# ScalarE instead of SP issues the store of a block's decoded weight words, behind its own cast of them

## The chip, the cores and the metric

The kernel runs on one core of one Trainium2 chip. The metric is device time of one launch in microseconds (us), the median of several runs. One more execution was taken by the hardware profiler; its rows are what this document reads.

## The reference

Attention over blocks, a gated causal convolution, a Fourier mix and a two-layer network, one after the other, for 8 batches of 576 positions and 512 channels:

```python
attn = softmax(scale * q @ k.T, block-causal mask of 64) @ v
x    = concat_heads(attn)                                   # (8, 576, 512)
x    = (sigmoid(causal_conv(x, conv_w)) * (x @ w_val)) @ w_out
mixed = real(fft(fft(x, axis=1), axis=2))
u  = x + mixed
un = (u - mean(u)) / sqrt(var(u) + 1e-6)
out = u + relu(un @ w_ch1) @ w_ch2                          # 512 -> 2048 -> 512
```

The weights come in as 64-bit floats. The kernel gets their 32-bit halves, and builds 32-bit floats from them on the chip.

## The kernel before

**Two phases.** `phase1` does attention, convolution and the Fourier mix, and writes u to DRAM (`u_d`). `phase2` does the normalization and the two-layer network. The first 1024 tokens (two groups g of 512) go through the network directly: for each of 16 blocks f of 128 hidden units, TensorE makes `psh` (12 matmuls of 512 columns, L1516 to L1518: three products of high and low parts for four slices of 128), ScalarE and VectorE turn it into `HL` (L1520 is the high part with the relu, L1521 the low part), and the 12 matmuls `o` (L1537 to L1539) add block f-1 to the output. The remaining tokens go through a scheme with fewer products, whose weight sums are built meanwhile by `combine` from the decoded blocks in DRAM.

**A block's weights.** Blocks 0 and 1 are decoded in phase 1. Blocks 2 to 15 are decoded by `load_w` while group 0 runs, with `load_raw` and `keep_base` around it:

- L1189: two loads of 512 KB bring the block's raw words (`rw`).
- L71: ScalarE makes the size of each word (`st`, 128x1024). `st` is one of three buffers.
- L75, L76, L80, L82: VectorE finishes `st`, in place.
- L1213: SP issues the store of `st` to DRAM (`w_d`, 512 KB). A buffer of `st` is free for L71 of the third block behind it when this store has landed and the block's L1216 is done.
- L1215: ScalarE casts `st` to the high parts, the first half of the block's weight tile `W`.
- L1216: VectorE makes the low parts, the other half of `W`.
- L1201: SP stores three of the four high and low pieces (`base_d`, 768 KB).

In `psh` of a block the first and second matmul of each slice need the high parts, the third (L1518) the low ones.

**What sets the order.** A scheduler decides, when the program is built, the order in which each engine's instructions stand, from its own estimate of times; every engine then works through its list in that order. SP's list holds nearly all DMAs. [...]

Of the kernel before, what the change touches and what calls it, by code (L numbers as in the profile page):

```python
# [17 lines left out]
def kernel(  # L18
# [13 lines left out]
    nc = tc.nc  # L32
# [32 lines left out]
    def decode(raw, dst, fine=False):  # L65

        lo, hi = raw[:, 0::2], raw[:, 1::2]
        d = dst.bitcast(I32)

        def size():  # L70
            nc.scalar.activation(out=dst, in_=hi.bitcast(F32), func=AF.Abs)  # L71

        def bits():

            nc.vector.tensor_scalar_max(out=dst, in0=dst, scalar1=2.0 ** -15)  # L75
            nc.vector.tensor_scalar(out=d, in0=d, scalar1=3, scalar2=0x3FFFFFFF,  # L76
                                    op0=ALU.logical_shift_left, op1=ALU.bitwise_and)

        def rest():
            nc.vector.scalar_tensor_tensor(out=d, in0=lo, scalar=29, in1=d,  # L80
                                           op0=ALU.logical_shift_right, op1=ALU.bitwise_or)
            nc.vector.scalar_tensor_tensor(out=d, in0=hi, scalar=-0x40000000, in1=d,  # L82
                                           op0=ALU.bitwise_and, op1=ALU.bitwise_or)

        def whole():
            bits()
            rest()
        return [size, bits, rest] if fine else [size, whole]
# [8 lines left out]
    w_d = [dram.tile([P, 2 * D], F32, name=f"w_d{f}") for f in range(NF)]  # L97
# [16 lines left out]
    def w_places(f, t):  # L114
        WQ[f] = [x[:, 0:D] for x in t]
# [934 lines left out]
    def phase2():  # L1050
        with ExitStack() as c2:
# [31 lines left out]
            def at(n, shape, dt, name):  # L1083
                return place[n].tile(shape, dt, tag="w", name=name)
# [120 lines left out]
            def load_w(f):  # L1205
                W = at(f, [P, 4 * D], F32R, f"W{f}")
                WW[f] = W
                w_places(f, [W[:, D * z:D * z + D] for z in range(4)])
                h, l = (W.rearrange("p (q y c) -> p q y c", y=2, c=256)[:, :, y] for y in range(2))
                st = s3.tile([P, 2 * D], F32, tag="st", name="st")  # L1210
                for stage in decode(RAW[f], st):
                    stage()
                nc.sync.dma_start(out=w_d[f], in_=st)  # L1213
                x = st.rearrange("p (q c) -> p q c", c=256)
                nc.scalar.copy(out=h, in_=x)  # L1215
                nc.vector.tensor_tensor(out=l, in0=x, in1=h.bitcast(F32), op=ALU.subtract)  # L1216

            pin = [False]
# [269 lines left out]
            for g in range(NG):  # L1488
# [4 lines left out]
                for f in range(NF + 1):  # L1493
# [3 lines left out]
                    if g == 0 and f + 2 < NF:  # L1497
                        load_raw(f + 5)
                        load_w(f + 2)
                        if f + 2 < NH:  # L1500
                            keep_base(f + 2)
# [177 lines left out]
```

## Time and profile before

| | |
|---|---|
| median of 3 runs | 1404.49 us (1403.73 to 1406.47) |
| profiled execution | 1408.24 us, its span 1406.2 us |
| TensorE (PE) busy | 1352.7 us, 96% of the span |
| VectorE (DVE) busy | 1087.7 us, 77% |
| ScalarE (ACT) busy | 821.8 us, 58% |
| store of decoded words (L1213) | 14 issues, 512 KB each, 655.4 to 757.9 us of the span |

The profiled execution is 3.75 us above the median of the runs. PE is TensorE's matmuls, PEld its weight loads, DVE VectorE, ACT ScalarE, POOL GpSimd, SP the engine that only issues. A name with q at its end (SPq) is an engine's queue of instructions that count as no busy time, such as DMA issues. "idle before" is the time that an engine stood still ahead of an instruction, with what ended it. In a list of order, a tile name ends in a number that tells one buffer's use from the next.

### The profile page before, as it was taken

The page shows a single profiled execution, that of the slowest core. Times are in us where ns is not written, and L with a number is a line of the kernel's source. Part 1 is how long each engine was busy: PE and PEld are TensorE (multiplying, and loading weights), DVE is VectorE, ACT ScalarE, POOL GpSimd, SP SyncE. Part 2 cuts the span into 40 slices and gives each one's busy share as a digit, 9 for nine tenths or more (in the row PEclk, how much of TensorE's full clock was granted, in tenths as well). Part 3 has the DMA queues.
Part 4 walks back from the last instruction along what each step waited for, and adds up shares of the span by engine and source line. Part 5 has one row for each costly group of instructions (what it writes and reads, how often), then busy time and mean ns, then how long its engine had stood idle before and what let it go on. Part 6 is the DMA issues. An engine that isn't in the chain of part 4 may idle for free.

```text
span 1406.2 us, 24032 instructions
## 1 busy us (share of the span) xinstructions
PE 1352.7 (96%) x8547; PEld 1188.0 (84%) x8547; DVE 1087.7 (77%) x1965; ACT 821.8 (58%) x1792; POOL 211.0 (15%) x186
## 2 busy tenths in 40 slices
PE   5798999999999999999999999999999999999998
PEld 3576789898999988888778788888888889999998
DVE  5867788787879797989889798599746983796374
ACT  5677867777777777774444344574356534744451
POOL 2423232323223232322200000000000000000000
PEclk9799999999999999999999999999999999999999
DMA  7566665656656566646698987985875579779875
GB/s 211 137 167 187 160 185 153 173 149 165 160 154 159 155 171 157 178 150 215 217 359 291 340 320 246 318 275 190 289 261 200 179 243 334 251 252 320 272 253 185
DMA packets 177043, 308.78 MB, mean 220 GB/s; under 512 B 28430, under 2 KB 107036, under 8 KB 169756
## 3 DMA queue, kind: packets, MB, share of 16 engines
q1 hardware_dynamic: 176096, 306.57, 69.1%
q8 instruction: 68, 1.11, 0.3%
q0 software_dynamic: 288, 0.53, 0.2%
q14 instruction: 51, 0.42, 0.1%
q10 hardware_dynamic: 540, 0.14, 0.1%
HBM read 204.27 MB, written 56.77 MB: 186 GB/s over the span
## 4 chain that ended last, share of the span: by engine, by line
PE 68%; DVE 14%; DMA 6%; ACT 4%; issue 3%; POOL 3%; SPq 1%; DVEq 0%; ACTq 0%; POOLq 0%
PE banks L1437 12%; PE banks L1438 12%; PE banks L1439 12%; PE av L616 4%; PE pt L588 4%; DVE gate L643 2%; PE sc L428 2%; POOL XA L849 2%; PE sc L429 2%; DVE mx L460 1%; PE psx L192 1%; PE psx L194 1%; PE psx L193 1%; DMA rw<-in_w_ch 1%; ACT PB L474 1%
## 5 line engine op out<-in xcount | busy, mean ns | idle before, releaser
L1437 PE MATMUL banks<-o,chunk 128*128 128x512 f32 (+1 forms) x896 | 324.2, 362 | 1.1 <-ACT h L1445 1.1
L1438 PE MATMUL banks<-o,chunk 128*128 128x512 f32 (+1 forms) x896 | 324.0, 362 | 0.0
L1439 PE MATMUL banks<-o,chunk 128*128 128x512 f32 (+1 forms) x896 | 324.0, 362 | 0.0
L474 ACT ACTIVATE PB<-sc,mx 128x128 f32<-128x128 f32 (+4 forms) x320 | 166.8, 526 | 49.6 <-DVE mx L460 27.7
L1437 PEld LDWEIGHTS banks<-o,chunk 128*128 128x128 f32 x896 | 168.2, 188 | 19.3 <-ACT h L1445 2.0
L1438 PEld LDWEIGHTS banks<-o,chunk 128*128 128x128 f32 x896 | 168.2, 188 | 17.4
L1439 PEld LDWEIGHTS banks<-o,chunk 128*128 128x128 f32 x896 | 168.2, 188 | 17.5
L1397 ACT CAST o<-h 128x1024 fp32r<-128x1024 f32 (+1 forms) x112 | 105.4, 945 | 106.9 <-PE banks L1439 86.5
L588 PE MATMUL pt<-ident,PB 128*128 128x128 f32 x800 | 142.9, 285 | 15.4 <-ACT PTb L594 8.2
L1398 DVE TENSOR_TENSOR o<-h,o 128x1024 fp32r<-128x1024 f32 (+1 forms) x112 | 119.8, 1084 | 23.6 <-ACT o L1397 23.2
L588 PEld LDWEIGHTS pt<-ident,PB 128*128 128x128 f32 x800 | 101.7, 145 | 32.5 <-ACT PTb L594 14.7
L643 DVE SCALAR_TENSOR_TENSOR gate<-XF,cw,gate 128x575 f32<-128x575 f32 (+3 forms) x128 | 122.7, 958 | 4.3 <-ACT gate L63 3.6
L460 DVE TENSOR_REDUCE mx<-sc 128x1 f32<-128x384 f32 (+2 forms) x192 | 104.3, 560 | 4.4 <-PE sc L194 2.7
L428 PE MATMUL sc<-K,QQ 128*128 128x256 f32 (+2 forms) x256 | 88.3, 355 | 14.4 <-DMA QQ<-QHL 13.5
L594 ACT COPY PTb<-pt 128x512 f32<-128x512 f32 (+1 forms) x160 | 86.7, 545 | 18.9 <-PE pt L588 18.2
L1445 ACT COPY h<-banks 128x1024 f32<-128x1024 f32 (+1 forms) x64 | 58.1, 907 | 56.9 <-PE banks L1439 56.9
L192 PE MATMUL psx<-GH,we_h 128*128 128x290 f32 x256 | 83.6, 326 | 2.5 <-ACT GH L57 1.5
L192 PE MATMUL psv<-XH,wv_h 128*128 128x288 f32 x256 | 83.8, 328 | 0.4 <-ACT PB L474 0.4
L639 POOL TENSOR_TENSOR XL<-XF,XH 128x576 fp32r<-128x576 f32 x32 | 45.9, 1434 | 251.1 <-ACT XH L57 250.9
L429 PE MATMUL sc<-KL,QQ 128*128 128x256 f32 (+2 forms) x256 | 83.3, 336 | 0.0
L193 PE MATMUL psx<-GL,we_h 128*128 128x290 f32 x256 | 76.1, 297 | 0.5 <-DVE GL L704 0.5
L193 PE MATMUL psv<-XL,wv_h 128*128 128x288 f32 x256 | 76.3, 298 | 0.0
(272 smaller groups left out, 3152.5 us busy)
## 6 DMA issues: line engine op xcount, KB each, us to landing
chunk<-comb_d SPq DMA_DIRECT2D x64, 512.0 KB, 5.8
chunk<-comb_d SPq DMA_DIRECT2D x32, 1024.0 KB, 4.8
chunk<-base_d SPq DMA_DIRECT2D x48, 512.0 KB, 5.9
chunk<-base_d SPq DMA_DIRECT2D x24, 1024.0 KB, 6.8
K<-KP SPq DMA_DIRECT2D x128, 144.0 KB, 2.5
QQ<-QHL SPq DMA_DIRECT2D x128, 128.0 KB, 2.4
rw<-in_w_ch SPq DMA_DIRECT2D x28, 512.0 KB, 8.2
comb_d<-packed SPq DMA_DIRECT2D x12, 1024.0 KB, 5.1
```

The source lines that it names most:

```text
L192: nc.tensor.matmul(ps, lh, rh, start=first, stop=False)
L193: nc.tensor.matmul(ps, lh, rl, start=False, stop=False)
L428: nc.tensor.matmul(t[:, o:o + w], q[:, 0, m], KK[p][h][:, 0:w], start=True, stop=False)
L429: nc.tensor.matmul(t[:, o:o + w], q[:, 1, m], KL[p][:, 0:w], start=False, stop=True)
L460: nc.vector.reduce_max(out=mx[:, j:j + 1], in_=t, axis=AX.X, negate=one)
L474: nc.scalar.activation(out=PB[i][:, k0:k0 + w], in_=t, func=AF.Exp, bias=nm, accum_out=su[:, at + j:at + j + 1])
L588: nc.tensor.transpose(ps[:, j, :], PB[i][:, (j0 + j) * P:(j0 + j + 1) * P], ident)
L643: nc.vector.scalar_tensor_tensor(out=gate[c][:, s:S], in0=XF[:, 0:S - s], scalar=cw[:, c, 4 - s:5 - s], in1=gate[c][:, s:S], op0=ALU.mult, ...
L1398: nc.vector.tensor_tensor(out=o[:, 1], in0=x, in1=o[:, 0].bitcast(F32), op=ALU.subtract)
L1437: nc.tensor.matmul(to, wh, o[:, 0, x], start=first, stop=False, skip_group_check=not begin)
L1438: nc.tensor.matmul(to, wh, o[:, 1, x], start=False, stop=False, skip_group_check=not begin)
L1439: nc.tensor.matmul(to, wl, o[:, 0, x], start=False, stop=last, skip_group_check=not begin)
```

## The change

The store moves from SP's list to ScalarE's, and in the program's text from ahead of the cast to behind it.

```diff
                 st = s3.tile([P, 2 * D], F32, tag="st", name="st")
                 for stage in decode(RAW[f], st):
                     stage()
-                nc.sync.dma_start(out=w_d[f], in_=st)
                 x = st.rearrange("p (q c) -> p q c", c=256)
                 nc.scalar.copy(out=h, in_=x)
+                nc.scalar.dma_start(out=w_d[f], in_=st)
                 nc.vector.tensor_tensor(out=l, in0=x, in1=h.bitcast(F32), op=ALU.subtract)
```

A line is taken out above the cast, so the cast is L1214 in the changed kernel and the store L1215. The scheduler orders all engines anew; outside this stage little moves.

First SP's list, at the raw words of blocks 10 to 14 of group 0. `w_d7` to `w_d10` are the stores of blocks 7 to 10, `rw_9629` is block 11's raw words, `rw_9669` block 12's, `rw_9709` block 13's, `rw_9749` block 14's. Before:

```order
L1213 DMA w_d7_78<-st_9592 128x1024
L1201 DMA base_d01_88<-W7_9591 128x3x512
L1189 DMA rw_9629<-in_w_ch1 128x4x256
L1189 DMA rw_9629<-in_w_ch2 128x1024
L1213 DMA w_d8_79<-st_9633 128x1024
L1189 DMA rw_9669<-in_w_ch1 128x4x256
L1189 DMA rw_9669<-in_w_ch2 128x1024
L1213 DMA w_d9_80<-st_9673 128x1024
L1189 DMA rw_9709<-in_w_ch1 128x4x256
L1189 DMA rw_9709<-in_w_ch2 128x1024
L1213 DMA w_d10_81<-st_9713 128x1024
```

And in the changed kernel:

```order
L1201 DMA base_d01_88<-W7_9591 128x3x512
L1189 DMA rw_9629<-in_w_ch1 128x4x256
L1189 DMA rw_9629<-in_w_ch2 128x1024
L1189 DMA rw_9669<-in_w_ch1 128x4x256
L1189 DMA rw_9669<-in_w_ch2 128x1024
L1189 DMA rw_9709<-in_w_ch1 128x4x256
L1189 DMA rw_9709<-in_w_ch2 128x1024
L1189 DMA rw_9749<-in_w_ch1 128x4x256
L1189 DMA rw_9749<-in_w_ch2 128x1024
```

The loads stand in the same order; the stores between them, each of which waited for VectorE, are gone.

Then ScalarE's list, at the casts of blocks 8 to 11. `st_9713` is block 10 in decoding, `st_9753` block 11, `st_9796` block 12; `psh_9682`, `psh_9722` and `psh_9765` are the first-layer sums of blocks 7, 8 and 9. Before:

```order
L1215 CAST W8_9632<-st_9633 128x4x256
L1520 ACTIVATE HL_9331<-psh_9682 128x512
L1215 CAST W9_9672<-st_9673 128x4x256
L71 ACTIVATE st_9713<-rw_9588 128x1024
L1520 ACTIVATE HL_9331<-psh_9722 128x512
L1215 CAST W10_9712<-st_9713 128x4x256
L1520 ACTIVATE HL_9331<-psh_9765 128x512
L71 ACTIVATE st_9753<-rw_9629 128x1024
L71 ACTIVATE st_9796<-rw_9669 128x1024
L1215 CAST W11_9752<-st_9753 128x4x256
```

And in the changed kernel:

```order
L1214 CAST W8_9632<-st_9633 128x4x256
L1215 DMA w_d8_79<-st_9633 128x1024
L71 ACTIVATE st_9713<-rw_9588 128x1024
L1520 ACTIVATE HL_9331<-psh_9682 128x512
L1214 CAST W9_9672<-st_9673 128x4x256
L1215 DMA w_d9_80<-st_9673 128x1024
L71 ACTIVATE st_9753<-rw_9629 128x1024
L1520 ACTIVATE HL_9331<-psh_9722 128x512
L71 ACTIVATE st_9796<-rw_9669 128x1024
L1214 CAST W10_9712<-st_9713 128x4x256
L1215 DMA w_d10_81<-st_9713 128x1024
L1520 ACTIVATE HL_9331<-psh_9765 128x512
```

Beside the stores, L71 of blocks 10, 11 and 12 has moved up: block 10's now stands ahead of the relu of block 7's sums, and block 12's ahead of the cast of block 10.

Last VectorE's list at the same place. Before:

```order
L82 SCALAR_TENSOR_TENSOR st_9713<-rw_9588,st_9713 128x1024
L1216 TENSOR_TENSOR W10_9712<-st_9713,W10_9712 128x4x256
L1521 SCALAR_TENSOR_TENSOR HL_9331<-psh_9765,HL_9331 128x512
L75 TENSOR_SCALAR st_9753<-st_9753 128x1024
L76 TENSOR_SCALAR st_9753<-st_9753 128x1024
L80 SCALAR_TENSOR_TENSOR st_9753<-rw_9629,st_9753 128x1024
L82 SCALAR_TENSOR_TENSOR st_9753<-rw_9629,st_9753 128x1024
```

And in the changed kernel:

```order
L82 SCALAR_TENSOR_TENSOR st_9713<-rw_9588,st_9713 128x1024
L1521 SCALAR_TENSOR_TENSOR HL_9331<-psh_9722,HL_9331 128x512
L75 TENSOR_SCALAR st_9753<-st_9753 128x1024
L75 TENSOR_SCALAR st_9796<-st_9796 128x1024
L1216 TENSOR_TENSOR W10_9712<-st_9713,W10_9712 128x4x256
L76 TENSOR_SCALAR st_9753<-st_9753 128x1024
L76 TENSOR_SCALAR st_9796<-st_9796 128x1024
L80 SCALAR_TENSOR_TENSOR st_9753<-rw_9629,st_9753 128x1024
L1521 SCALAR_TENSOR_TENSOR HL_9331<-psh_9765,HL_9331 128x512
L82 SCALAR_TENSOR_TENSOR st_9753<-rw_9629,st_9753 128x1024
```

The first step of blocks 11 and 12 now stands ahead of the low parts of block 10.

## Rows read from the trace of the kernel before

**Rows 1.** The profile page: the span, and the engines' busy time.

```profile
span 1406.2 us, 24032 instructions
PE 1352.7 (96%) x8547; PEld 1188.0 (84%) x8547; DVE 1087.7 (77%) x1965; ACT 821.8 (58%) x1792; POOL 211.0 (15%) x186
```

**Rows 2.** Busy time by stage: PE, PEld, DVE, ACT, POOL, clock, DMA share, GB/s.

```profile
690.00:742.00 52.00, 51.06 (x220) 40.54 (x219) 44.89 (x52) 22.93 (x26) 1.10 (x2) 1.00 1.03 354
742.00:766.00 24.00, 24.00 (x107) 19.32 (x106) 23.25 (x32) 11.47 (x17) 0.00 (x0) 1.00 0.80 275
766.00:800.00 34.00, 34.00 (x150) 27.87 (x150) 25.88 (x49) 11.00 (x16) 1.61 (x3) 1.00 0.94 325
880.00:1406.00 526.00, 521.38 (x2618) 471.46 (x2616) 368.18 (x441) 253.85 (x307) 0.00 (x0) 1.00 0.75 255
```

**Rows 3.** Timeline of PE, 660 to 810 us: the instructions with idle time ahead.

```profile
667.09 0.73 PE L1516 MATMUL psh<-UTH,K 128*128 128x512 f32 x2 [0.42 <-ACT UTH L1135]
668.24 0.50 PE L1517 MATMUL psh<-UTL,K 128*128 128x512 f32 x1 [0.41 <-DVE UTL L1136]
681.99 0.73 PE L1539 MATMUL o<-HL,KP 128*128 128x512 f32 x2 [0.56 <-DVE HL L1521]
...
729.08 0.50 PE L1518 MATMUL psh<-UTH,W 128*128 128x512 f32 x1 [0.52 <-DVE W L1216]
...
734.61 0.50 PE L1516 MATMUL psh<-UTH,W 128*128 128x512 f32 x1 [0.21 <-ACT W L1215]
735.99 0.50 PE L1518 MATMUL psh<-UTH,W 128*128 128x512 f32 x1 [0.17 <-DVE W L1216]
...
802.33 0.49 PE L1114 MATMUL pm<-ah,ones 128*128 128x512 f32 x1 [1.12 <-ACT ah L1111]
```

**Rows 4.** Waits of ACT and of SP's queue, 690 to 770 us: total, times, longest.

```profile
ACT st L71 <- DMA w_d<-st: 4.7, 3, 2.3
...
SPq L1213 <- DVE st L82: 28.0, 7, 5.8
```

**Rows 5.** The decoded words' tile w_d: issue ns min/median/max, and landing times.

```profile
L1213 SPq DMA_DIRECT2D w_d<-st x14: 319/336/2851, 655.4 to 757.9; - x14
...
DMA to landing us min/median/max: 3.1/4.7/7.7
```

**Rows 6.** DMA, 715 to 735 us: packets, and issues with median us to landing.

```profile
DMA packets 3924, 7.80 MB, mean 390 GB/s; under 512 B 242, under 2 KB 2362, under 8 KB 3921
...
rw<-in_w_ch SPq DMA_DIRECT2D x6, 512.0 KB, 11.7
w_d<-st SPq DMA_DIRECT2D x4, 512.0 KB, 7.7
```

**Rows 7.** Timeline of ACT: the relu of block 7, and decoding of blocks 10 to 12.

```profile
714.60 0.60 ACT L1520 ACTIVATE HL<-psh 128x512 fp32r<-128x512 f32 x1
...
721.11 1.13 ACT L71 ACTIVATE st<-rw 128x1024 f32<-128x1024 f32 x1 [1.17 <-DMA w_d<-st]
...
726.71 1.05 ACT L1215 CAST W<-st 128x1024 fp32r<-128x1024 f32 x1 [3.99 <-DVE st L82]
...
730.53 1.15 ACT L71 ACTIVATE st<-rw 128x1024 f32<-128x1024 f32 x1 [1.24 <-DMA w_d<-st]
```

**Rows 8.** Timeline of PE: the first matmul that needs block 7's relu.

```profile
719.78 0.39 PE L1537 MATMUL o<-HL,W 128*128 128x512 f32 x1
```

**Rows 9.** Timeline of DVE, 727 to 734 us: low parts of block 10, decoding of 11.

```profile
727.79 1.23 DVE L1216 TENSOR_TENSOR W<-st,W 128x1024 fp32r<-128x1024 f32 x1 [1.11 <-ACT W L1215]
728.94 0.68 DVE L1521 SCALAR_TENSOR_TENSOR HL<-psh,HL 128x512 fp32r<-128x512 f32 x1
...
730.26 0.70 DVE L76 TENSOR_SCALAR st<-st 128x1024 int32<-128x1024 int32 x1
730.99 1.23 DVE L80 SCALAR_TENSOR_TENSOR st<-rw,st 128x1024 int32<-128x1024 int32 x1
732.25 1.22 DVE L82 SCALAR_TENSOR_TENSOR st<-rw,st 128x1024 int32<-128x1024 int32 x1
```

## The prediction, made before the changed kernel ran

> **What bounds the kernel now.** I read the page first: PE is busy 1352.7 of 1406.2 us [rows 1], so time can only come from PE's stalls or go into new ones. Then the busy time by stage, where the change acts: stores are issued from 655 to 758 us [rows 5]. From 690 to 742 us the DMA engines have a share of 1.03, so their queue is never empty; DVE is busy 44.89 of 52 us, ACT 22.93, and PE 51.06 [rows 2]. From 742 to 766 us DVE is the fullest, 23.25 of 24, and PE does not stand still. So this stage first lives on DMA, then on DVE, and PE keeps up with little to spare. PE's timeline gives the stalls: 0.42, 0.41 and 0.56 us before 690, then 0.52, 0.21 and 0.17 us on the weights of blocks 10 and 11, then 1.12 us at 802 [rows 3]. Blocks 10 and 11 cost 0.90 us, all seven 3.41 us. That is all there is to gain here. The clock is full in every stage [rows 2].
>
> Why were blocks 10 and 11 late? ACT's L71 waited 4.7 us, three times, for the store of an earlier block to free its buffer of st [rows 4]; for block 10 until 721.11, for block 12 until 730.53 [rows 7].
>
> **What the change removes.** SP no longer waits for VectorE ahead of a store: 28.0 us in seven waits [rows 4]. I price this at nothing, since the DMA engines were full meanwhile; a load issued sooner only stands longer in the queue (11.7 us from issue to landing [rows 6]). Without that cover it would be worth no more than the 0.90 us, because PE waited for no other thing there.
>
> **What it adds.** Fourteen issues on ACT. No DMA is issued by ACT in this trace, so the nearest row is the same store on SP: 0.336 us median, 0.319 to 2.851 [rows 5]. At the median that is 4.7 us of ACT's time, and 29 of 52 us are idle there [rows 2]; I take 0, with 4.7 us if none of it were covered. The store also starts one cast later (1.05 us [rows 7]), and leaves SP's queue. On SP's queue it took 7.7 us to land in the full stretch [rows 6], at best 3.1 [rows 5]. With a queue of its own I take a landing nearer to 3.1 to 5 us, so L71's wait for a store goes. That is worth between 0 and 0.90 us, by itself.
>
> But it doesn't make loads land sooner. The same bytes pass through the same full engines; a store that came behind the loads of the next blocks now passes them. One store is 0.524 MB, at 390 GB/s [rows 6] 1.34 us. In the old queue block 9's store stood right behind block 12's words and landed at about 730.5 (it released L71 [rows 7]); so those words landed at about 729.15. In the changed kernel block 9's store can pass them: 729.15 if it doesn't, 730.5 if it does. I take 730.5: block 9's cast, behind the relu of block 7 (below), ends by about 725, four microseconds before, and the transfer is short.
>
> [...]
>
> **What it moves.** This is the term that decides. The scheduler expected the buffers earlier and put L71 of block 10 ahead of the relu of block 7, and L71 of block 12 ahead of the cast of block 10 (the lists above). ACT works through its list in order, so these now wait for raw words which nothing makes earlier.
>
> - Relu of block 7: before at 714.60 [rows 7], needed by PE at 719.78 [rows 8]. L71 of block 10 began at 721.11. Its words stood in front of block 7's store, so they landed about 1.34 us sooner, 719.7; now the stores of blocks 7 and 8 can both pass them: 721.0 to 722.4. With 1.13 for L71 and 0.60 for the relu, PE gets block 7 at 722.8 to 724.1, 3.0 to 4.3 us late. Queued behind it: the cast of block 9 and its store.
> - Cast of block 10: L71 of block 12 at 730.5, plus 1.15, plus the cast 1.05, plus the low parts 1.23 [rows 7, 9], with some 0.1 between them: 734.0. Before, the low parts ended at 729.0 (727.79 + 1.23) and PE went on at 729.08 [rows 3]. So PE is 5.0 us late at block 10; with 729.15, 3.6. The first delay is within this one, not on top of it: PE only arrives later at the same wait.
> - Block 11: VectorE has, behind block 10's low parts, two L76 (0.70 each), L80, L1521 and L82 (1.23, 0.68, 1.22 [rows 9]): 738.5. Then comes the cast on ACT, and L80 of block 12 and L75 of block 13 on VectorE (1.23 + 0.7, about 740.4), then the low parts: 741.6, some overlap of starts taken off 741.5. Before, PE went on at 735.99 [rows 3]: 5.5 us late.
> - After that neither engine has room to catch up: PE has no idle time from 742 to 800 and VectorE is nearly full to 766 [rows 2]. I carry 5.5 us on.
> - The stall of 1.12 us at 802 waits for an input load (x of the next part) that doesn't depend on PE; PE comes there about 5 us later, so it goes: -1.1. If VectorE's delay passes on to that load, it stays.
>
> From 880 us on PE is busy 521.38 of 526 [rows 2], and nothing there is gained or lost.
>
> **Sum.** +5.5 - 1.1 + 0 (issues) = +4.4 us. The gain of 0.90 us is already in it, since block 10 and 11 are compared with their old stalled times. Against the profiled execution: 1408.24 + 4.4 = 1412.6. That execution was 3.75 us above the median of the runs, so for a median of runs I say 1404.49 + 4.4 = 1408.9 us, 0.31% slower.
>
> **Rivals.**
>
> 1. *No change that can be told* (within 0.2%, 2.8 us, about what a measurement of this kernel can tell). It needs block 12's words some 2 us before 729.15. For: the stage's mean is 354 GB/s [rows 2] and 390 in its second half [rows 6]; 373 from 690 on, 5% more over 39 us, would do it, and two queues could mix loads and stores better. Against: the share is full already. Then PE loses 0 to 2 us more, and 1.1 come back: 1404 to 1407. [...]
> 2. *Faster.* It takes the same earlier words, by over 3.6 us: L71 of block 12 has to start by 725.5 (726.71 less 1.15 and the handover) for the cast not to be later than before. Then stores no longer hold L71, VectorE has work between the last decode step and the low parts (the lists above), and blocks 10 and 11 don't stall: -0.90, with the 1.12 at 802 and the 0.56 at 682 gone too -2.6, with all seven -3.4: 1401 to 1403.6. For: 7 us of idle VectorE from 690 to 742 [rows 2]. Against: that idle time is mostly waiting for words and casts, and the words don't come sooner.
> 3. *ACT is held at its stores.* Some stores on ACT wait for a semaphore that a load or store of SP had before (block 12's store for block 14's words). If that lands late, the relu behind it waits, and PE with it. Words took 11.7 us to land [rows 6]; block 14's were issued at least that long before block 12's cast, so I expect 0. If an issue costs ACT 2.85 us [rows 5] in the full stretch, or a store waits 3 us, PE loses about 5 more: 1414.
>
> **Chances.** Forecast (2.8 to 8 us slower) 0.52; no change 0.30; faster by over 0.2% 0.10, the rest of rival 2 being within the second case; held at stores 0.08. So faster 0.10, same 0.30, slower 0.60. The likeliest case alone runs from 1407.3 to 1412.5. The range reaches down into the case of no change, to 1403.0, leaving some 0.12 below, and up to 1414.0, leaving 0.08.
>
> **What would show it.** Right: L71 of block 12 on ACT ends its wait on a load of words, at about 730, and the cast of block 10 comes right behind it, at 731 to 733 instead of 726.71; PE has new stalls of 2 to 5 us in all between 718 and 742 on the relu of block 7 and the weights of block 10; L71 waits for no store any more; the stores land in 3 to 5 us; DMA is as full as before. Wrong: if L71 of block 12 starts by 727, the stage's DMA does better with two queues than with one; if PE's stalls up to 760 stay near 1 us in all, the order did no harm; if ACT's time is lost at its issues, the third rival holds.

## The result, and the profile after

The changed kernel takes 1411.82 us (median of 5 runs, 1409.36 to 1412.78), the kernel before 1404.49 (1402.84 to 1406.55) beside it: 1.0051 times as long, 95% interval 1.0040 to 1.0062, so 7.3 us slower. Forecast were 1408.9 us, 4.4 us slower, in a range of 1403.0 to 1414.0.

The page of the profiled execution (span, busy time; beside [rows 1]), then busy time by stage (columns as in [rows 2]):

```profile
span 1410.9 us, 24024 instructions
PE 1353.1 (96%) x8547; PEld 1188.7 (84%) x8547; DVE 1088.4 (77%) x1965; ACT 822.7 (58%) x1792; POOL 210.1 (15%) x186
```

```profile
690.00:742.00 52.00, 48.92 (x198) 37.56 (x199) 42.49 (x49) 21.80 (x25) 1.10 (x2) 0.97 1.04 371
742.00:766.00 24.00, 21.00 (x92) 16.70 (x91) 22.08 (x31) 11.49 (x17) 0.00 (x0) 1.00 0.88 319
```

All engines do the work that they did. The DMA engines are as full as before (1.04), but PE is busy 48.92 of 52 us where it was 51.06, 21.00 of 24 where it was 24.00, and the granted clock of the first stretch is 0.97.

The two profiled spans differ by 4.7 us only, since the profiled execution of before had taken longer ahead of this stage. TensorE runs 8547 matmuls in both; number 4896 (counted from 0) starts at 651.35 us before and 2.34 us earlier after. I count from there: how much later each matmul starts than the one of the same number in the kernel before, beyond that offset. The last one comes 7.06 us later, near the 7.3 us between the medians. On the way (in the table under the experiments): -0.60 at 691 us of the clock of before, +4.46 at 743, +7.92 at 757, 7.96 at 798, 6.56 at 805, 7.06 at the end. So 5.06 us are lost on blocks 6 to 12, 3.46 us right behind them, 1.40 come back at 802.

TensorE's timeline after, the instructions with idle time ahead (in brackets), to be read beside [rows 3]:

```profile
707.18 0.50 PE L1539 MATMUL o<-HL,W 128*128 128x512 f32 x1 [0.48 <-DVE HL L1521]
718.19 0.50 PE L1537 MATMUL o<-HL,W 128*128 128x512 f32 x1 [0.28 <-ACT HL L1520]
722.52 0.50 PE L1518 MATMUL psh<-UTH,W 128*128 128x512 f32 x1 [0.57 <-DVE W L1216]
...
729.63 0.50 PE L1516 MATMUL psh<-UTH,W 128*128 128x512 f32 x1 [1.03 <-ACT W L1214]
730.89 0.50 PE L1518 MATMUL psh<-UTH,W 128*128 128x512 f32 x1 [0.53 <-DVE W L1216]
...
754.23 0.49 PE L1114 MATMUL pm<-ah,ones 128*128 128x512 f32 x1 [1.67 <-ACT ah L1111]
757.44 0.50 PE L1115 MATMUL pm<-al,ones 128*128 128x512 f32 x1 [1.32 <-DVE al L1112]
...
805.31 0.40 PE L1114 MATMUL pm<-ah,ones 128*128 128x512 f32 x1
```

A low part of HL at 707 us, the relu of block 7 and the weights of blocks 9 and 10 stop TensorE. Then pm does, the sums for the next group's normalization, which it did not wait for before: L1114 needs ah, the high part that ScalarE makes, L1115 al, the low part that VectorE makes. The 1.12 us at 802 are gone. The stall at 707 us costs 0.90 us (-0.60 to 0.30 in the table, from 691 to 711 us). It goes back to block 7's words, which landed 2.25 us later than before (below): L71 of block 7 waited for them, and VectorE's steps of block 7 stand ahead of this L1521. The busy time in stretches of 4 us shows one thing more:

```profile
728.00:732.00 4.00, 2.44 (x9) 1.40 (x8) 3.08 (x5) 2.08 (x3) 0.00 (x0) 0.94 1.07 369
732.00:736.00 4.00, 4.00 (x13) 3.17 (x12) 4.00 (x6) 1.57 (x2) 0.00 (x0) 0.64 1.05 396
736.00:740.00 4.00, 4.00 (x19) 3.29 (x18) 4.00 (x6) 2.02 (x3) 0.00 (x0) 1.00 1.05 412
```

Behind the stalls at 729 to 731 us the clock granted to TensorE is lower, 0.75 from 731 to 732 us, 0.50 from 732 to 734, 0.54 from 734 to 735, and 1.00 again from 735 on: 13 matmuls in 4 us where the next stretch has 19. The two stretches lack 0.06 and 0.36 of 4 us, 1.7 us in all, and those are part of the 5.06.

ScalarE's timeline, beside [rows 7]:

```profile
716.53 1.12 ACT L71 ACTIVATE st<-rw 128x1024 f32<-128x1024 f32 x1 [4.19 <-DMA rw<-in_w_ch]
717.56 0.58 ACT L1520 ACTIVATE HL<-psh 128x512 fp32r<-128x512 f32 x1
...
727.52 1.12 ACT L71 ACTIVATE st<-rw 128x1024 f32<-128x1024 f32 x1 [2.26 <-DMA rw<-in_w_ch]
728.54 1.04 ACT L1214 CAST W<-st 128x1024 fp32r<-128x1024 f32 x1
...
734.43 1.16 ACT L71 ACTIVATE st<-rw 128x1024 f32<-128x1024 f32 x1 [4.35 <-DMA w_d<-st]
```

L71 of block 10 waits for its words with the relu of block 7 behind it, L71 of block 12 with the cast of block 10 behind it; L71 of block 13 then waits for the store of block 10. The clock of this stage is 2.94 us ahead of before's (the offset at 691 us), so 727.52 is 730.46 there. ScalarE's waits from 690 to 770 us (beside [rows 4]), the stores' issues (beside [rows 5]) and DMA from 715 to 735 us (beside [rows 6]):

```profile
ACT st L71 <- DMA rw<-in_w_ch: 13.5, 5, 4.2
ACT st L71 <- DMA w_d<-st: 7.8, 3, 4.4
```

```profile
L1215 ACTq DMA_DIRECT2D w_d<-st x14: 326/326/376, 653.2 to 758.6; - x14
```

```profile
DMA packets 4577, 7.70 MB, mean 385 GB/s; under 512 B 746, under 2 KB 3239, under 8 KB 4575
...
rw<-in_w_ch SPq DMA_DIRECT2D x5, 512.0 KB, 10.6
w_d<-st ACTq DMA_DIRECT2D x3, 512.0 KB, 7.1
```

No store holds ScalarE (326 ns each, none above 376), but on a queue of their own (q10: 1.57 MB from 715 to 735 us; before, loads and stores were all on q1) they land in 7.1 us, hardly sooner than in 7.7 before, and L71 waits for them longer (7.8 us for 4.7). When words and stores landed (last part of each transfer, from the trace's records; after with 2.94 us added, the run with the stores on ScalarE in the old order, below, with 4.63):

```
landed at, us       before   after   ScalarE, old order
words of block 7    700.02   702.27   701.67
store of block 5    704.12   701.57   700.64
words of block 10   719.11   719.37   718.66
words of block 11   725.20   726.46   725.86
words of block 12   729.16   730.35   729.03
store of block 7    721.00   716.68   716.35
store of block 9    730.43   730.07   727.06
store of block 10   734.38   737.27   736.16
```

### The profile page after: what moved, and what is told of

The parts are those of the page before. It is cut to its first block, busy times and chain, and to the rows that moved or that the text cites. A ratio compares the mean times of both kernels' runs of the same rounds, so it can differ in the third digit from the quotient of the medians.

```text
span 1410.9 us, 24024 instructions
## 1 busy us (share of the span) xinstructions
PE 1353.1 (96%) x8547; PEld 1188.7 (84%) x8547; DVE 1088.4 (77%) x1965; ACT 822.7 (58%) x1792; POOL 210.1 (15%) x186
## 4 chain that ended last, share of the span: by engine, by line
PE 69%; DVE 13%; DMA 7%; ACT 4%; issue 3%; POOL 2%; SPq 1%; DVEq 0%; ACTq 0%; POOLq 0%
PE banks L1437 12%; PE banks L1438 12%; PE banks L1439 12%; PE av L616 4%; PE pt L588 4%; DMA rw<-in_w_ch 2%; DVE gate L643 2%; PE sc L428 2%; PE sc L429 2%; POOL XA L849 1%; DVE mx L460 1%; PE psx L192 1%; ACT PB L474 1%; DMA comb_d<-packed 1%; PE psx L194 1%
```

## Experiments

Theory ORDER: the time is lost because the scheduler, which expects the buffers of st earlier, puts L71, low parts and pm elsewhere in the engines' lists. Theory QUEUE: it is lost because stores on a second queue run beside the loads of words. To part them, several kernels end with a list of instructions by engine, and each is tied behind its neighbour in issue order, without a wait (shortened):

```
for engine, at, *steps in ORDER:
    last = f"I-{at}"
    for step in steps:
        at += step
        tc.add_manual_dep(by[f"I-{at}"], last, NoSync, reason="order")
        last = f"I-{at}"
```

The lists (763 instructions of TensorE, 291 of VectorE, 143 of ScalarE, 109 of SP, those between the first and the last difference) are taken from the kernel before (old) or the changed one (new). Built, the programs stand in these orders but for two neighbouring matmuls of block 0 (in ACT,old, pinned, SP,new and PE old of the table) and one store to base_d, of block 6 (in ACT,old and pinned). The times' ratios are to the kernel before, run on the same chip beside each. The table has TensorE's lateness in the profiled execution of each, in us beyond its offset at matmul 4896 (n: number of the matmul; before: its start there). Each column is one execution, and its last row lies up to 2.1 us from the difference of the medians (NL13: 8.96 against 6.86; ACT,old: 1.75 against 3.30); what is read from it is the loss between two rows of one column:

```
   n   before  changed  ACT,old  pinned  POOL,old  POOL>6  SP,new  PE old  SP old  ahead  3 back  4 back  rule   NL13
5124   691.56   -0.60   -0.03    0.04    2.24     0.07   -0.06    0.17   -0.15  -0.80   0.11   -0.46  -0.53  -0.61
5208   710.94    0.30    1.25    1.37    3.76     0.10    0.21    1.73    0.81  -0.31   1.09    0.39  -0.87   0.10
5244   719.10    0.31    1.25    1.37    3.76     8.29    0.50    1.73    0.82  -0.27   1.11    0.40  -0.87   0.11
5268   724.54    2.06    1.25    1.37    3.76     8.33    4.93    3.53    2.20   3.25   1.11    0.40   2.17   5.25
5304   733.56    5.71    0.39    0.52    2.91     7.47    5.40    5.53    5.85   3.61   3.83    2.95   1.33   6.52
5340   743.00    4.46    2.19    1.94    2.80     7.05    5.41    5.38    4.58   4.03   3.72    2.92   3.14   6.54
5400   756.78    7.92    2.19    1.97    2.80     7.05    6.98    9.32    6.30   4.43   7.19    6.32   3.81  10.28
5580   798.11    7.96    2.19    1.99    2.80     7.31    7.02   10.71    6.29   4.31   7.23    6.36   3.77  10.18
5604   804.98    6.56    1.60    1.76    2.99     8.05    5.63    9.35    9.19   2.91   5.84    4.97   3.60   8.78
8546  1401.77    7.06    1.75    2.50    3.76     8.30    4.12    8.77    8.43   2.04   4.91    5.95   3.27   8.96
```

**Stores on ScalarE, old order** (ACT,old):

```
 nc.scalar.dma_start(out=w_d[f], in_=st)   # as in the changed kernel
+keep_order(tc)                            # all lists as before
```

> The stores stay on ScalarE, but TensorE, VectorE, ScalarE and SP work through their lists in the order of the kernel before (edges of issue order between neighbours, no waits). Theory ORDER (the loss comes from where the scheduler put L71, the low parts and pm): 1403 to 1406 us, no clock below 1.00 from 690 to 760 us, TensorE idle under 1 us on blocks 7 to 11 and on pm. Theory QUEUE (the loss comes from the stores running on a second queue beside the loads): 1409 to 1413, with blocks 10 and 11 late although nothing stands ahead of their casts.

Measured: 1406.76 us against 1403.46, ratio 1.0022 (1.0012 to 1.0031), 3.1 us, between the ranges of both theories. Neither alone: most of the loss is gone, not all. TensorE's stalls that are new against [rows 3], and ScalarE's timeline at the store of block 10:

```profile
703.14 0.50 PE L1518 MATMUL psh<-UTH,W 128*128 128x512 f32 x1 [1.18 <-DVE W L1216]
...
731.58 0.50 PE L1516 MATMUL psh<-UTH,W 128*128 128x512 f32 x1 [1.39 <-ACT W L1214]
```

```profile
722.19 1.05 ACT L1214 CAST W<-st 128x1024 fp32r<-128x1024 f32 x1 [4.07 <-DVE st L82]
724.43 0.33 ACTq L1215 DMA_DIRECT2D w_d<-st  x1
724.85 0.60 ACT L1520 ACTIVATE HL<-psh 128x512 fp32r<-128x512 f32 x1 [1.62 <-DMA rw<-in_w_ch]
```

Two costs of the queue. Block 7's words land 1.65 us later than before, since the store of block 5 lands ahead of them (the landings above); VectorE's list has L75, L76 and L80 of block 7 ahead of block 6's low parts, so TensorE stands 1.18 us for these (the expectations below call it the stall on block 7's weights). And ScalarE stands 1.6 us at the store of block 10, which goes out at 724.43 us, as block 12's words land (729.03 less 4.63). That the two share a semaphore is my reading and not shown; the trace has the wait and what ended it. One gain: the stall on block 10 goes (1.25 to 0.39 in the table).

**Stores on SP, new order** (SP,new):

```
-nc.scalar.dma_start(out=w_d[f], in_=st)   # behind the cast
+nc.sync.dma_start(out=w_d[f], in_=st)
+keep_order(tc)                            # all lists as in the changed kernel
```

Without the last line every engine's list comes out as before, so the place behind the cast alone changes no order (this was built and not timed).

> The stores stay on SP, but the four engines work in the order of the changed kernel. Theory ORDER: 1410 to 1414 us, with the stalls of the changed kernel: about 2.5 us on the relu of block 7 and the weights of blocks 9 and 10, a stretch at half clock behind them, and 3.0 us on pm (L1114, L1115). Theory QUEUE: 1403 to 1406, as before.

Measured: 1409.26 us, ratio 1.0038 (1.0026 to 1.0051), 5.3 us, 0.7 us under the range of theory ORDER. The stall on pm is 1.33 us in place of the 3.0 forecast. The lists alone cost more than the queue alone (ACT,old), by 743 us as much as both together: 5.47 us from matmul 5124 to 5340, 5.06 in the changed kernel, 2.22 with the queue alone. In all, lists and queue together cost 7.3 us against a sum of 8.4, which the intervals (1.4 to 1.8 us to each side) allow to be the same. TensorE, and ScalarE's L71 of block 10, which now waits for the store of block 7 on SP's queue:

```profile
719.85 0.50 PE L1537 MATMUL o<-HL,W 128*128 128x512 f32 x1 [2.23 <-ACT HL L1520]
...
756.05 0.50 PE L1115 MATMUL pm<-al,ones 128*128 128x512 f32 x1 [1.33 <-DVE al L1112]
```

```profile
718.20 1.12 ACT L71 ACTIVATE st<-rw 128x1024 f32<-128x1024 f32 x1 [5.70 <-DMA w_d<-st]
719.21 0.59 ACT L1520 ACTIVATE HL<-psh 128x512 fp32r<-128x512 f32 x1
```

Here, too, the clock falls behind the stall (0.70 and 0.87 in the stretches from 720 and 724 us, 1.7 us again).

**Each store pinned behind its cast, old order** (pinned): the first of these kernels, with the stores of blocks 3 to 15 in ScalarE's list, each behind its cast.

> As the run with the stores on ScalarE in the old order, but each store stands right behind its cast on ScalarE's list (there, the store of block 12 stood ahead of a relu and of its own cast, and ScalarE stood still 3.2 us at it). Theory HOLD (what the second queue costs in the old order is ScalarE standing still at stores): the late relu at 736 us goes, the store of block 10 still waits for the semaphore of block 12's words (1.6 us): 1405 to 1406.5 us. Theory PASS (it costs because stores pass words that ScalarE needs next): nothing changes, 1406 to 1408, with the stall of 1.2 us on block 7's weights at 703 us as before.

Measured: 1407.42 us against 1403.64, ratio 1.0027 (1.0019 to 1.0036), no better: in PASS's range, over HOLD's. From matmul 5304 to 5340 1.42 us are lost in place of 1.80, so the late relu had cost some 0.4; the stalls on blocks 6 and 11 stay (1.18 and 1.61 us).

**Stores on GpSimd, old order** (POOL,old): `nc.gpsimd.dma_start`, lists as before.

> Stores issued by GpSimd, all other engines in the old order, so that no engine of the decoding stands still at a store. Theory HOLD: no loss, 1402.5 to 1404 us. Theory PASS: the store of block 5 still lands ahead of block 7's words and TensorE still stands 1.2 us on block 7's weights, 0.8 us of blocks 10 and 11 come back: 1404 to 1405. If a queue on another engine is slower in itself, stores land later than 7 us and L71 waits for them: over 1406.

Measured: 1407.11 us, ratio 1.0024 (1.0016 to 1.0033). TensorE's stalls at the same two places:

```profile
705.28 0.50 PE L1518 MATMUL psh<-UTH,W 128*128 128x512 f32 x1 [1.18 <-DVE W L1216]
...
733.80 0.50 PE L1518 MATMUL psh<-UTH,W 128*128 128x512 f32 x1 [0.26 <-DVE W L1216]
```

The same 1.18 us on block 6 with another engine as issuer, and no stall on block 11's cast: the first belongs to the queue, the second to ScalarE standing at a store. The time is over both forecasts, since 2.2 us were lost at 660 to 672 us, with a granted clock of 0.57 from 664 to 668; why stays open. The third forecast, a slower queue, has the time but not for its reason: L71 waited for no store from 690 to 770 us.

**Stores on SP up to block 6, on GpSimd from 7 on, old order** (POOL>6):

```
-nc.scalar.dma_start(out=w_d[f], in_=st)   # as in the changed kernel
+(nc.gpsimd if f > 6 else nc.sync).dma_start(out=w_d[f], in_=st)
+keep_order(tc)                             # all lists as before
```

> Old order; SP issues the stores of blocks 2 to 6, GpSimd those from block 7 on. Theory PASS (in the old order the cost is the store of block 5 landing ahead of block 7's words): the stall of 1.2 us on block 7's weights is gone, the 0.8 us of block 10 stay won, and so do GpSimd's first stores cost nothing at 664 to 672 us: 1402 to 1404 us, at or just under the kernel before. Rival (any second queue slows the loads): 1405 to 1408, as with all stores on GpSimd.

Measured: 1413.24 us against 1405.04, ratio 1.0061 (1.0049 to 1.0074). The stall on block 6 is gone (0.10 at matmul 5208), as PASS has it, and so is the loss at 664 to 672. The time says nothing on the rest: the buffers of st are dealt out when the program is built, and here alone block 9 got the buffer of block 7, not of block 6, so its L71 stood 10.65 us for the store of two blocks before, and TensorE 5.29 for the cast of block 8 behind it:

```profile
716.72 1.12 ACT L71 ACTIVATE st<-rw 128x1024 f32<-128x1024 f32 x1 [10.65 <-DMA w_d<-st]
```

**Store on ScalarE ahead of the cast** (ahead; lists free): the engine alone is changed.

```
-nc.sync.dma_start(out=w_d[f], in_=st)
+nc.scalar.dma_start(out=w_d[f], in_=st)
```

> ScalarE issues the store, but it is written ahead of the cast as before: the engine alone is changed, and the scheduler is free. The place alone (SP issues it, written behind the cast) leaves every engine's list as it was. Theory ENGINE: L71 moves up as in the changed kernel and the time is 1409 to 1413 us. Rival (the place behind the cast matters, since a store ahead of it lets the buffer go a microsecond sooner): 1404 to 1407.

Measured: 1407.00 us, ratio 1.0023 (1.0014 to 1.0033). The rival is right in size, but not for its reason: the scheduler made a third set of lists, in which TensorE stands 2.18 us on block 9's low parts and loses almost nothing on pm (4.03 to 4.43). Which place in the text is better is decided by the lists that come out.

**Three instructions put back** (3 back): new lists, but

```
ScalarE:  L71 of block 10 behind the relu of block 7
          L71 of block 12 behind the cast and store of block 10
VectorE:  L1216 of block 10 ahead of L75 of block 12
```

> The changed kernel with three instructions put back in the lists, all else as in it: on ScalarE, L71 of block 10 behind the relu of block 7 and L71 of block 12 behind the cast and store of block 10; on VectorE, the low parts of block 10 ahead of L75 of block 12. Theory ORDER: TensorE's loss from block 6 to block 12 falls from 5.1 us to 2.5 or less, with no stretch at half clock, and the later loss on pm (3.5 us), if it is the same lateness handed on, falls too: 1404.5 to 1407.5 us. Rival (the second queue is what makes blocks 9 to 11 late): 1409 to 1412.

Measured: 1408.74 us against 1405.04, ratio 1.0031 (1.0019 to 1.0042), over ORDER's range and just under the rival's; up to block 12 TensorE loses 3.6 us, where ORDER had 2.5 or less. It passes block 7 without loss and then stands at the relu of block 8, which waits behind L71 of block 11; pm is as before the edit:

```profile
725.09 0.50 PE L1537 MATMUL o<-HL,W 128*128 128x512 f32 x1 [3.02 <-ACT HL L1520]
...
751.42 0.50 PE L1114 MATMUL pm<-ah,ones 128*128 128x512 f32 x1 [1.68 <-ACT ah L1111]
754.63 0.50 PE L1115 MATMUL pm<-al,ones 128*128 128x512 f32 x1 [1.32 <-DVE al L1112]
```

**Four put back** (4 back): L71 of block 11 behind the relu of block 8, too.

> As the run with three instructions put back, and on ScalarE L71 of block 11 behind the relu of block 8, too (with three put back, TensorE stood 3.0 us on that relu, which waited behind L71 for block 11's words). Theory ORDER: no relu waits behind a L71 any more; the 3.0 us and the 0.9 behind it go: TensorE's loss up to block 12 under 1.5 us; the wait on pm stays if VectorE's list is late by its own order, and goes if it was lateness handed on: 1405 to 1407.5 us against 1404 to 1405 of before, or 1404 to 1405. Rival (block 11's words land some 2 us late on account of the second queue, and the casts of blocks 10 and 11 are late with them in whatever order): no better than 1408 to 1409.

Measured: 1408.53 us against 1403.68, ratio 1.0032 (1.0020 to 1.0044), as the rival has it. No relu is late now, but up to block 12 TensorE still loses 3.4 us, on blocks 10 and 11, where ORDER had under 1.5. This does not show the queue alone to be the cause: L71 of block 11, whose words land 1.4 us later than before, still stands ahead of the cast of block 10 on ScalarE, where the old list has it behind:

```profile
724.22 1.12 ACT L71 ACTIVATE st<-rw 128x1024 f32<-128x1024 f32 x1 [5.28 <-DMA rw<-in_w_ch]
...
725.24 1.04 ACT L1214 CAST W<-st 128x1024 fp32r<-128x1024 f32 x1
```

On pm it loses

```profile
752.13 0.50 PE L1114 MATMUL pm<-ah,ones 128*128 128x512 f32 x1 [1.67 <-ACT ah L1111]
755.33 0.50 PE L1115 MATMUL pm<-al,ones 128*128 128x512 f32 x1 [1.31 <-DVE al L1112]
```

the same 3.0 us as with one and a half more of lateness ahead of it (3.46, 3.47 and 3.40 us in the table for the changed kernel, three and four back). So these are not TensorE's lateness of blocks 10 and 11 handed on. They come with the lists: 0.0 in the four runs with the old ones, also in the one that comes there 7.05 us late (POOL>6).

**Three edits on the wait for pm**, each on the changed kernel:

```
PE old:  keep_order(tc) with TensorE's old list and the new ones of ScalarE, VectorE and SP
SP old:  keep_order(tc) with SP's old list and the new ones of TensorE, ScalarE and VectorE
NL13:    -NL = 12
         +NL = 13    # lists free
```

> The changed kernel, with TensorE alone in the order of before (pm of the next group a block later, psh and o woven as before); ScalarE, VectorE and SP keep the new order. If the 3.5 us that the changed kernel loses at 750 to 758 us come from pm standing earlier on TensorE: 1408 to 1409 us, the waits on L1114 and L1115 gone and the loss on blocks 7 to 10 unchanged (about 5 us up to 742 us). Rival: VectorE is late anyway, and TensorE waits the same 3 us a little later, on weights of blocks 13 to 15: 1411 to 1413.

> The changed kernel with SP alone in its old order, so that the stores of blocks 8 to 11 to base_d (768 KB each) are issued after the loads of combine again and not at 739 to 747 us, among the stores that L71 of blocks 13 to 15 waits for. Theory BASE (those late stores of decoded words delay VectorE and give the 3.5 us at 750 to 758): L71 waits for stores under 4 us in place of 7.8, the stalls on pm fall under 1.5 us, 1408.5 to 1410 us. Rival (VectorE's list is late by itself after block 10): 1411 to 1413, pm stalls of 3 us as before.

> The changed kernel with the normalization of the next group started one block later (NL 13 for 12), the scheduler free. Theory PM (3.5 us of the loss are pm standing on TensorE ahead of al): the stalls on L1114 and L1115 before 770 us go and nothing takes their place: 1407.5 to 1409.5 us. Rival (VectorE is late there anyway, and TensorE waits as long for weights of blocks 13 to 15): 1411 to 1413.

Measured: 1412.90 us, ratio 1.0061 (1.0048 to 1.0073); 1412.44, 1.0060 (1.0047 to 1.0073); 1411.90, 1.0049 (1.0035 to 1.0063). None wins anything; the times are the rivals' (1411 to 1413). In turn, TensorE's stall near 755 us in the first, two of the second, one of the third:

```profile
751.33 0.50 PE L1539 MATMUL o<-HL,W 128*128 128x512 f32 x1 [2.12 <-DVE HL L1521]
```

```profile
755.63 0.50 PE L1115 MATMUL pm<-al,ones 128*128 128x512 f32 x1 [1.33 <-DVE al L1112]
806.27 0.50 PE L1115 MATMUL pm<-al,ones 128*128 128x512 f32 x1 [2.41 <-DVE al L1112]
```

```profile
761.43 0.50 PE L1115 MATMUL pm<-al,ones 128*128 128x512 f32 x1 [1.55 <-DVE al L1112]
```

With pm back in its old place TensorE waits for VectorE's L1521 instead (2.12 us), and the clock granted behind it is 0.61 and 0.97 in the stretches from 752 and 756 us (3.9 us lost from matmul 5340 to 5400). With two of the four stores to base_d late again the loss there halves (1.72 us from matmul 5340 to 5400), as expected, and it is 1.57 in the run with the stores on SP, whose queue holds the stores to base_d back too; but L71 waits for stores as long as before (7.9 us in four) and 2.9 us are lost at 802. With NL 13 the wait goes along with pm (3.7 us), but its lists differ elsewhere, too: TensorE stands 3.00 us on the relu of block 7.

**A rule in place of a list** (rule; NL 13): L71 of block f only behind the cast of block f-2 and the relu of block f-3.

```
...
+for e in (("cast", f - 2), ("relu", f - 3)):
+    if e in ISSUED:
+        behind(made, ISSUED[e])     # made: L71 of block f
...
```

> Stores on ScalarE; L71 of a block may stand on ScalarE's list only behind the cast of two blocks before and the relu of three blocks before; the normalization of the next group starts one block later (NL 13 for 12), so that pm stands behind psh of block 14. Theory ORDER: the loss is gone, and with L71 no longer waiting for stores perhaps the 0.9 us of before too: 1402 to 1405 us. Theory QUEUE: 1409 to 1413, since the stores still run beside the loads.

Measured: 1407.09 us, ratio 1.0023 (1.0013 to 1.0033), between the ranges of both theories: TensorE no longer waits for pm before 770 us, but the cast and the low parts of block 9 (1.53 and 0.92 us) and, later, the low parts of block 12 (1.96 us) are late, with 1.7 us lost to a clock of 0.64 and 0.93 in the stretches from 740 and 744 us. No kernel tried beats the one before.

## Why the prediction was right, and where its size was off

**What the removed waits and the added issues are worth: nothing. Right.** Between 690 and 770 us no wait of ScalarE in the changed kernel is at a store. With the store gone from SP's queue, words landed no sooner: block 12's at 730.35 on the clock of before, forecast 730.5, before 729.16. Block 5's store, which came 4.1 us behind block 7's words on one queue, now lands 0.7 us ahead of them. The DMA engines' share hardly moved (1.03 and 1.04), and yet the queue alone cost 3.1 us in the old order. One premise was wrong: in the trace of before ScalarE does issue DMAs, 27 of 5 KB at L504, in 280 ns each (median); the stores take it 326.

**The stores' own landing. Wrong.** I took 3 to 5 us and no wait of L71 for a store. They landed in 7.1 us in the full stretch, and L71 waited 7.8 us for three. Only in the old order did the gain that I had bounded by 0.90 appear: 0.85 us on block 10, in four runs. The bound itself was read too small: 0.90 us is TensorE's idle time alone. Counted from start to start against the 0.23 us of an undisturbed matmul, the stalls on blocks 10 and 11 cost 1.7 us.

**L71 ahead of the relu of block 7. Right in place, too large.** TensorE was to be 3.0 to 4.3 us late; it went on at 718.19, which is 721.13 on the clock of before, 1.35 us after [rows 8], and 0.90 of that had been lost at 707 us already, which stood in no term of mine. I had let the stores of blocks 7 and 8 pass block 10's words and delay them by 1.34 us each. Block 7's did pass them (716.68), block 8's did not (722.70), and the words landed at 719.37, only 0.26 us later than before.

**L71 of block 12 ahead of the cast of block 10. Right.** L71 at 730.46 (forecast 730.5), the low parts released TensorE at 730.89, so 733.83 (forecast 734.0). The lists do this without the second queue (5.47 us by 743 us with the stores on SP). Putting back the three instructions moved the loss to the next relu, so this kind of order stood in more places than the two that I had priced; with the fourth put back 3.4 us remained, and what of them is queue and what order is not shown. Up to 743 us 5.06 us were lost where I had 5.5, and that is luck in part: 0.90 of them fell at 707 us and 1.7 are the lower clock (0.50 from 732 to 734 us), neither in any term of mine, so that about 2.5 us are left for all that I had priced. Block 11, where I had the 5.5, did not stop TensorE at all.

**"After that neither engine has room to catch up ... I carry 5.5 us on." This step failed.** I carried the lateness through 742 to 760 us as a constant. TensorE lost 3.46 us more there, on ah and al. This term was short by half of the loss. In the new lists TensorE comes to pm earlier (within o of block 12, before within o of block 13), and VectorE makes al behind L80 of block 15, before ahead of its L76. VectorE's timeline, first of the kernel before, then of the changed one:

```profile
753.13 0.68 DVE L1112 TENSOR_TENSOR al<-s,ah 128x512 fp32r<-128x512 f32 x1
```

```profile
756.70 0.69 DVE L1112 TENSOR_TENSOR al<-s,ah 128x512 fp32r<-128x512 f32 x1
```

756.70 is 759.64 on the clock of before, 6.5 us later, while TensorE itself was 4.5 us late and has the matmul on al 10 places earlier in its list, the one on ah 12. With the old lists the loss is absent, in four runs; with the new ones and the stores on ScalarE it is there to 0.1 us, in three runs; with the stores to base_d later, half of it, in two. That is what the sum lacked.

**The stall at 802. Right:** forecast -1.1, measured -1.40. The rest after 805 us (+0.5) was not forecast. Sum, with -0.60 ahead of 691 us and 0.04 between 757 and 798: 5.06 + 3.46 - 1.40 + 0.50 - 0.60 + 0.04 = 7.06.

**Rivals.** No change and faster needed earlier words; they came later. ScalarE held at its stores did not happen in the changed kernel, and did in the old order, at the store of block 10, until block 12's words landed, a wait of the kind that I had named: 1.6 us there. From matmul 5304 to 5340 TensorE lost 1.80 us (pinned 1.42), and nothing with GpSimd as issuer.

Left open: how much of VectorE's lateness comes from L71 of blocks 13 to 15 waiting 7.8 us for stores, which the prediction had at nothing; why the 3.46 us halve when stores to base_d are later; and why the loss then comes up again at 802 us.

## What to carry to other kernels

Before pricing a DMA moved to another engine, put the new lists of all engines beside the old ones as far as anything differs, and price each consumer that moved ahead of its producer; here the lists cost 5.3 us by themselves and the queue 3.1. Here the second queue let late transfers land ahead of early ones (block 5's store 0.7 us ahead of block 7's words): good where the buffer of a store was waited for (0.85 us on block 10), bad where the words that were passed fed the decoding (1.18 us on block 6). One engine's old list among new ones won nothing (1412.90 and 1412.44 us against 1411.82, within the intervals). And a forecast near the result is not yet a mechanism: of the 5.06 us up to 743 about half were priced.

## What the runs showed of the hardware

- A store of 512 KB on a queue of its own landed in 7.1 us in the full stretch, in 7.7 among the loads; the DMA engines' mean rate rose from 354 [rows 2] to 371 GB/s over 690 to 742 us, and the words that the decoding waited for came up to 2.25 us later.
- The clock granted to TensorE, in two stretches of 4 us at and behind a stall: 0.70 and 0.87 behind 2.23 us (stores on SP in the new order), 0.61 and 0.97 behind 2.12 (TensorE in the old), 0.83 and 0.74 behind 2.18 (store ahead of the cast), 0.87 and 0.70 behind 3.00 (NL 13), and in the changed kernel 0.94 and 0.64 behind 1.03 and 0.53 us close together. What they lack of 1.00 comes to 1.7 us each time. Not behind every such stall: with three instructions put back TensorE stood 3.02 us at 722 to 725 us and every stretch up to 772 us had a clock of 1.00.
- An issue took 326 ns on ScalarE, 336 on SP [rows 5], 540 on GpSimd (medians of 14).
